# Row loads held until the MLP passes, five more x blocks by crossbar in batches 1 and 2, and a reordered front for batch 0

## The chip, the cores and the metric

The kernel runs on one NeuronCore of a Trainium2 chip. The metric is device time in microseconds (us). One NeuronCore has TensorE (PE, matrix products into PSUM), VectorE (DVE), ScalarE (ACT), GpSimd (POOL), SyncE (SP), each with its own in-order instruction queue, and 16 DMA engines that the queues share. Here GpSimd issues all loads from memory (software descriptors), and SP issues the outputs, small copies between on-chip tiles, and the transposes by the DMA crossbar.

## What is computed

Two stages, one after the other. First, chunked attention with memory: 4 batches, 8 heads, 768 positions, head size 64. Queries come in chunks of 32; each sees 8 memory keys and the keys from 16 before the chunk to 8 behind it.

```python
for c in range(nc):                                  # 24 chunks of 32
    q_c   = q[:, :, c*32 : c*32 + 32]
    k_ctx = k[:, :, max(0, c*32 - 16) : min(S, c*32 + 40)]
    scores = scale * q_c @ concat([mem_k, k_ctx]).T
    a = softmax(scores)
    out[:, :, chunk] = a @ concat([mem_v, v_ctx])
```

Second, on x, the attention's output as 3072 tokens of 512 values, an MLP with a "snake" activation:

```python
h = x @ w_in                       # 512 -> 2048
s = sin(alpha * h)
g = h + s * s / (alpha + 1e-9)
out = g @ w_out                    # 2048 -> 512
```

## The kernel before

One batch at a time goes through an attention stage and an MLP pass, and the second matmuls of a batch (by w_out) are fed, piece by piece, into the stages of the next one.

**Attention.** Keys and queries lie transposed in `kTs` and `qTs`, two buffers that alternate by batch; values lie in `vws`, alternating too. A block `j` is 96 queries (three chunks) with 128 keys: 16 before, 40 more, 8 memory keys, 64 more. For batches 1 to 3 `attention` runs the blocks 0 to 7: `scores` (TensorE, then three Exp instructions on ScalarE), two steps later `values` (TensorE, then `rinv` and `x_blk` on VectorE), and then the block's result is turned into `xT`. This is done by `turn_x`, four TensorE transposes and a VectorE copy, or, for the first `crossed` blocks, by one crossbar transpose on SP's queue (line 467). Before, `crossed` is 0 in batches 1 and 2 and 5 in batch 3. A number of second matmuls of the batch before, from the list `shares`, is put between the steps.

**Batch 0's front.** `attention_first` works by pairs of heads. Per pair: `turn_k`, `turn_q` (TensorE transposes and copies by ScalarE and VectorE), `sc` (scores of two halves and one Exp each), `pv` (values, `rinv`, `x_blk`) and `x` (transposes and a ScalarE copy). `warm(n)` issues n dummy matmuls on zeroes. All pairs' scores come first, then all values.

**The MLP pass.** `layer` goes through 16 steps `ft`: 8 first matmuls (line 483), Sin (line 503) on ScalarE, a square on VectorE, GpSimd or ScalarE by the letters V, P, A of a string, and the sum with h on VectorE (line 513). `second` holds the matmuls by w_out (line 529); its result is copied from PSUM into `o_sb` and sent out by SP. While `attention` runs, ScalarE makes this copy; otherwise VectorE and ScalarE take turns.

**Loads.** Batches 0 and 1 load k and q by `load_qk` and turn them on TensorE (`pair_up`, `turn`). Batches 2 and 3 load rows by `load_rows` (16 loads of k rows into `kst`, 6 of q rows into `qst`), and `cross_steps` turns each of the 14 tiles by a crossbar transpose on SP's queue into `kTs`, `qTs`. Before, the rows of batch 2 are loaded ahead of batch 1's attention, and its k tiles are crossed from that attention's fourth step on; the q tiles follow at the start of MLP pass 1. The rows of batch 3 are loaded after MLP pass 1, and all its 14 crossings are issued together in MLP pass 2 at step `ft` = 2. V of a batch is loaded just after the attention before it (`load_v`, four loads), and its memory rows are put in by eight small copies on SP (`send_memv`).

The order on every engine is the order in which the program calls; nothing is rescheduled. A load on GpSimd's queue waits for the landing of the eighth load before it.

Of the kernel before, what the change touches and what calls it, by code (L numbers as in the profile page):

```python
# [42 lines left out]
def kernel(  # L43
# [77 lines left out]
    memkT = consts.tile([P, HP, 32], BF, name="memkT")  # L121
    w_in_sb = consts.tile([P, KT, d_ff], BF, name="w_in_sb")
    w_out_sb = consts.tile([P, FT, d_model], BF, name="w_out_sb")
    ident_f = consts.tile([FT, FT], F32, name="ident_f")
    alpha_sb = consts.tile([P, FT], F32, name="alpha_sb")
    inv_alpha = consts.tile([P, FT], F32, name="inv_alpha")
# [3 lines left out]
    def alloc_qk():  # L130
        kb = qkst.tile([P, H, 6, D], BF, name="k_bf")
        qb = qkst.tile([P, H, 6, D], BF, name="q_bf")
        return kb, qb

    def load_rows(b):
        for j in range(NJ):
            lo = QW * j - 16
            r0 = max(0, -lo)
            nc.gpsimd.dma_start(  # L139
                kst[r0:64, j, :].rearrange("p (h d) -> p h d", d=D),  # L140
                k[b, :, lo + r0:lo + 64, :].rearrange("h p d -> p h d"),
            )
            n = min(56, S - (QW * j + 48))
            nc.gpsimd.dma_start(  # L144
                kst[72:72 + n, j, :].rearrange("p (h d) -> p h d", d=D),
                k[b, :, QW * j + 48:QW * j + 48 + n, :].rearrange("h p d -> p h d"),
            )
        nc.sync.dma_start(
            kst[64:72], memk_st[64:72, b - 2, :].unsqueeze(1).to_broadcast([NM, NJ, H * D])
        )  # L150
        for t in range(NSUB):
            nc.gpsimd.dma_start(  # L152
                qst[:, t, :].rearrange("p (h d) -> p h d", d=D),
                q[b, :, P * t:P * t + P, :].rearrange("h p d -> p h d"),
            )

    def cross_steps(b):
        for j in range(NJ):
            nc.sync.dma_start_transpose(kTs[b % 2][:, :, P * j:P * j + P], kst[:, j, :])
            yield  # L160
        for t in range(NSUB):
            nc.sync.dma_start_transpose(qTs[b % 2][:, :, P * t:P * t + P], qst[:, t, :])  # L162
            yield

    def load_qk(b, bufs, h0, h1):
        for src, dst in ((k, bufs[0]), (q, bufs[1])):
# [4 lines left out]

    def load_v(b, parts=((0, H),)):
        vw = vws[b % 2][:].rearrange("p h j c -> p (h j) c")
        vf = v[b].rearrange("h (j t) d -> t (h j) d", t=QW)
        n = H * NJ
        if len(parts) > 1:
            load_v_edges(vw, vf, n)
        for h0, h1 in parts:
            c0, c1 = h0 * NJ, h1 * NJ
            nc.gpsimd.dma_start(vw[16:64, c0:c1, 0:D], vf[0:48, c0:c1])  # L180
            nc.gpsimd.dma_start(vw[72:120, c0:c1, 0:D], vf[48:96, c0:c1])
        if len(parts) == 1:
            load_v_edges(vw, vf, n)

    def load_v_edges(vw, vf, n):
        nc.gpsimd.dma_start(vw[0:16, 1:n, 0:D], vf[80:96, 0:n - 1])
        nc.gpsimd.dma_start(vw[120:128, 0:n - 1, 0:D], vf[0:8, 1:n])

    def put_memv(b, eng, h0, h1):
        eng.tensor_copy(  # L190
# [188 lines left out]
    def attention_first(kq, alphas, ahead):  # L379
        xT = xp.tile([P, KT, S], BF, name="xT")  # L380
        pt, xb = {}, {}

        def turn_k(hp):
            t = turn(kq[0], hp, None)
            put_k(0, hp, t)
            put_k_edges(0, hp, t)

        def turn_q(hp):
            put_q(0, hp, turn(kq[1], hp, None))

        def sc(hp):
            for half in range(2):
                pt[hp, half] = unit_scores(hp, half)

        def pv(*u):
            xb[u] = unit_values(*u, pt[u])

        def x(*u):
            unit_turn(xT, *u, xb.pop(u))

        turn_k(0)
        warm(2)
        turn_q(0)
        mt = packed(single(), HP, 32)
        for g in range(HP):
            nc.tensor.transpose(mt[:, g, :], memk_bf[0:32, 2 * g:2 * g + 2, :].rearrange("p e d -> p (e d)"), ident[0:32, 0:32])
        nc.vector.tensor_copy(memkT[:], mt)
        put_memk(0)
        warm(3)
        turn_k(1)  # L410
        warm(2)
        sc(0)
        turn_q(1)
        alphas()
        put_memv(0, nc.vector, 0, H)
        warm(2)
        turn_k(2)
        warm(2)
        sc(1)
        turn_q(2)  # L420
        turn_k(3)
        warm(4)
        turn_q(3)
        sc(2)
        warm(2)
        sc(3)
        nc.scalar.preload_act_table(ACTF.Sin)
        send_memv(1)
        plan(big=(4, 0, 2), one=(6, 7))
        units = [(hp, half) for hp in range(HP - 1) for half in range(2)]  # L430
        pv(0, 0)
        for n in range(1, len(units)):
            warm(1)
            pv(*units[n])
            warm(1)
            x(*units[n - 1])
        warm(1)
        pv(3, 0)
        x(2, 1)
        pv(3, 1)  # L440
        x(3, 0)
        ahead(0, 0, xT)
        ahead(1, 0, xT)
        x(3, 1)
        ahead(2, 0, xT)
        return xT
# [73 lines left out]
    def second(i, gT, cut=0):  # L520

        def begin_o():
            bank = take_bank("one")
            kept.add(bank)
            return bank

        def part(s, bank, f0, f1):
            for ft in range(f0, f1):
                nc.tensor.matmul(  # L529
                    ps[:, bank, :], gT[:, ft, P * s:P * s + P], w_out_sb[:, ft, :],  # L530
                    start=(ft == 0), stop=(ft == FT - 1),
                )
                if ft < FT - 1:
                    yield

        def end_o(s, bank):
            kept.remove(bank)
            rings["one"].remove(bank)
            rings["one"].append(bank)
            o_sb = mlp.tile([P, d_model], F32, name="o_sb", bufs=2)  # L540
            if s % 2 == 0 and not state["attending"]:
                nc.vector.tensor_copy(o_sb[:], ps[:, bank, :])  # L542
            else:
                nc.scalar.copy(o_sb[:], ps[:, bank, :])  # L544
            nc.sync.dma_start(out[S * i + P * s:S * i + P * s + P, :], o_sb[:])

        early = []
        if cut:
            for s in range(2):
                early.append(begin_o())  # L550
                yield from part(s, early[s], 0, cut)
        for s in range(NSUB):
            bank = early[s] if s < len(early) else begin_o()
            yield from part(s, bank, cut if s < len(early) else 0, FT)
            end_o(s, bank)
            yield
# [15 lines left out]
        nc.vector.memset(vw[96:128, H - 1, NJ - 1, 0:D], 0.0)  # L572
    load_qk(0, kq, 0, 2)
    masks.make_identity(nc, ident[:])
    for hp in range(1, HP):
        load_qk(0, kq, 2 * hp, 2 * hp + 2)
    load_v(0, [(2 * hp, 2 * hp + 2) for hp in range(HP)])
    nc.gpsimd.dma_start(memv_st[64:72, 1:B].rearrange("n b h d -> n (b h) d"),
                        mem_v[1:B].rearrange("b h n d -> n (b h) d"))
    for kT in kTs:  # L580
        nc.vector.memset(kT[:, :, 0:16], 0.0)
        nc.vector.memset(kT[:, :, 848:856], 0.0)
# [37 lines left out]
    xT = attention_first(kq, alphas, ahead)  # L620
    for c in range(2):
        load_w_out(c)
    kq1 = alloc_qk()
    load_qk(1, kq1, 0, H)
    for bb in range(2):
# [29 lines left out]
    def begin_0(ft):  # L655
        if ft == 3:
            plan(h=[6] + rings["big"])
        if ft == 11:
            load_v(1)
        if ft == 15:  # L660
            prs.extend(pair_up(kq1[0], n) for n in range(3))

    layer(0, xT, "VPPAPAVPPAPAVAAA", begin_0, 0)
    last4 = rings["h"]
# [2 lines left out]
    feed.take(20)  # L667
    for pc in range(2 * HP):
        hp = pc % HP
        if pc + 3 < 2 * HP:  # L670
            prs.append(pair_up(kq1[(pc + 3) // HP], (pc + 3) % HP))
        t = turn(None, hp, prs[pc])
        if pc < HP:
            put_k(1, hp, t)
            put_k_edges(1, hp, t)
        else:
            put_q(1, hp, t, hp % 2 == 1)
        feed.take(2)
    nc.scalar.preload_act_table(ACTF.Exp)
    feed.take(4)  # L680
    load_rows(2)
    crossings = cross_steps(2)
    xT = attention(1, feed, (6, 8, 4, 4, 4, 3, 3, 3, 3, 1, 1), 2, 0, crossings, 3)
    load_v(2)
    send_memv(2)

    for i in range(1, B):
        last = i == B - 1
        if i > 1:
            crossings = cross_steps(i + 1) if not last else iter(())  # L690

        def begin(ft, i=i):
            if ft == (2 if i > 1 else 0):
                for _ in crossings:
                    pass

        if i == 1:
            assert feed.left() == 16
# [5 lines left out]
            plan(h=rings["big"])  # L704
            layer(i, xT, "AAAV", begin, feed.left() - (0 if last else 16))
        if not last:
            if i + 2 < B:
                load_rows(i + 2)
            plan(big=rings["h"])
            nc.scalar.preload_act_table(ACTF.Exp)  # L710
            feed.take(6)
            xT = attention(i + 1, feed, (4, 8, 4, 4, 3, 3, 3, 3, 4, 4, 4), 2, 5 if i == B - 2 else 0)
            if i + 2 < B:
                load_v(i + 2)
                send_memv(i + 2)
    feed.take(200)


# [28 lines left out]
```

The softmax here doesn't subtract the row's maximum and nothing guards it: scores larger than these inputs give would overflow.

## Time and profile before

| | |
|---|---|
| median of 6 runs | 226.04 us (225.82 to 226.6) |
| the profiled execution | 225.83 us, span 224.0 us |
| TensorE busy | 212.0 us (95%) |
| ScalarE busy | 152.4 us (68%) |
| VectorE busy | 132.9 us (59%) |
| GpSimd busy | 84.4 us (38%) |
| granted TensorE clock | 0.997 on average |

Times in the profile count from the span's start. The stages of batch 0's front end at about 27 us, MLP pass 0 at 49, the attention of batch 1 at 76, of batch 2 at 116, of batch 3 at 164; the last second matmuls run to 220. A line such as "L483 PE MATMUL ps<-xT,w_in_sb" names a line of the kernel, the engine, the operation, the tile written and those read. In the list of waits, "PE ps L483 <- DVE gT L513: 1.5, 5, 0.5" says that TensorE's line 483 waited for VectorE's line 513 for 1.5 us in all, 5 times, at most 0.5. Busy times of TensorE are modelled from the starts of its matmuls, and a few per cent of its records are missing, so busy is not the same as full speed.

### The profile page before, as it was taken

The numbers are of one execution on the slowest core, as the hardware profiler recorded it, in microseconds if no ns is written. First come the engines' busy times: TensorE is split into PE (matmuls) and PEld (weight loads), VectorE is DVE, ScalarE is ACT, GpSimd is POOL, SyncE is SP. The second block draws the span as 40 slices with busy tenths as digits, with TensorE's granted clock in tenths as the row PEclk, the third lists the DMA queues.
The fourth block names the chain that finished last, engine by engine and source line by source line (L and its number), as shares of the span: only waits on it lengthen the run. The fifth ranks groups of instructions, "written<-read, shape, count | busy, mean of one in ns | idle before, by whom it ended". The sixth has DMA issues, their size and how long they took to land.

```text
span 224.0 us, 4432 instructions
## 1 busy us (share of the span) xinstructions
PE 212.0 (95%) x1694; PEld 115.8 (52%) x1720; DVE 132.9 (59%) x234; ACT 152.4 (68%) x226; POOL 84.4 (38%) x106
## 2 busy tenths in 40 slices
PE   7998999999998999999999999999999999999992
PEld 2555555555545655554665555544555555544440
DVE  5684748793516869995682875756644863861110
ACT  2559478894787689999846879798929678651011
POOL 7969743796989941184980000000000000000000
PEclk9999999999999999999999999999999999999998
DMA  5999999999999999999999945542230110111211
GB/s 80 169 128 141 191 208 206 205 201 126 111 206 113 175 123 173 100 142 113 168 183 108 86 95 108 104 142 82 60 111 0 50 47 0 48 51 47 94 68 72
DMA packets 94573, 25.97 MB, mean 116 GB/s; under 512 B 82632, under 2 KB 91480, under 8 KB 94552
## 3 DMA queue, kind: packets, MB, share of 16 engines
q0 software_dynamic: 71520, 14.81, 113.6%
q1 hardware_dynamic: 23032, 10.88, 23.2%
q8 instruction: 13, 0.21, 0.5%
q14 instruction: 8, 0.07, 0.1%
HBM read 29.67 MB, written 6.29 MB: 161 GB/s over the span
## 4 chain that ended last, share of the span: by engine, by line
PE 66%; DVE 10%; ACT 7%; DMA 6%; issue 4%; SPq 3%; POOL 1%; DVEq 0%; ACTq 0%; POOLq 0%
PE ps L529 31%; PE ps L483 22%; DVE gT L513 6%; SPq L162 3%; ACT u L503 3%; DVE u L510 3%; DMA kT<-kst 3%; PE ps L296 3%; PE ps L270 2%; PE ps L323 2%; DMA q_bf<-in_q_dram 2%; PE ps L234 1%; PE ps L328 1%; PE ps L313 1%; ACT u L507 1%
## 5 line engine op out<-in xcount | busy, mean ns | idle before, releaser
L529 PE MATMUL ps<-w_out_sb,gT 128*128 128x512 bf16 x362 | 94.6, 379 | 1.5 <-ACT o_sb L544 0.4
L483 PE MATMUL ps<-xT,w_in_sb 128*128 128x384 bf16 x512 | 91.2, 326 | 1.6 <-DVE gT L513 1.5
L513 DVE SCALAR_TENSOR_TENSOR gT<-u,inv_alpha,ps 128x768 bf16<-128x768 f32 x64 | 63.3, 1012 | 24.0 <-ACT u L507 20.0
L483 PEld LDWEIGHTS <-w_in_sb 128*128 128x128 bf16 x512 | 49.6, 98 | 39.0 <-issue 3.2
L503 ACT ACTIVATE u<-ps,alpha_sb 128x768 f32<-128x768 f32 x64 | 56.6, 895 | 18.5 <-PE ps L483 17.6
L529 PEld LDWEIGHTS <-gT 128*128 128x128 bf16 x384 | 34.3, 98 | 30.9 <-issue 0.9
L507 ACT ACTIVATE u<-u 128x768 f32<-128x768 f32 x40 | 33.7, 843 | 1.2
L283 ACT ACTIVATE pt<-ps,biasm 128x256 bf16<-128x256 f32 x72 | 28.6, 480 | 5.0 <-ACT pt L283 2.6
L544 ACT COPY o_sb<-ps 128x512 f32<-128x512 f32 x16 | 9.4, 589 | 25.5 <-PE ps L529 25.5
L510 DVE TENSOR_TENSOR u<-u 128x768 f32<-128x768 f32 x18 | 17.2, 954 | 6.0 <-ACT u L503 6.0
L542 DVE COPY o_sb<-ps 128x512 f32<-128x512 f32 x8 | 5.5, 690 | 20.0 <-PE ps L529 17.2
L303 DVE TENSOR_TENSOR x_blk<-ps,rinv 96x512 bf16<-96x512 f32 x24 | 16.5, 687 | 0.8
L144 POOL DMA_DIRECT2D kst<-in_k_dram x16 | 11.7, 731 | 11.3 <-DMA vw<-in_v_dram 4.5
L302 DVE RECIPROCAL rinv<-ps 96x8 f32<-96x8 f32 x24 | 4.9, 203 | 17.0 <-ACT pt L283 10.7
L323 PE MATMUL ps<-idle 128*128 128x512 bf16 x35 | 12.0, 429 | 1.6 <-DVE vw L571 1.2
L139 POOL DMA_DIRECT2D kst<-in_k_dram x16 | 11.1, 694 | 6.2 <-DMA vw<-in_v_dram 5.2
L249 ACT COPY kT<-ps 128x672 bf16<-128x672 bf16 x8 | 5.7, 719 | 9.4 <-PE ps L234 6.6
L510 POOL TENSOR_TENSOR u<-u 128x768 f32<-128x768 f32 x6 | 8.9, 1494 | 6.9 <-ACT u L503 6.9
L296 PEld LDWEIGHTS <-pt 128*128 128x128 bf16 x192 | 9.0, 98 | 4.6 <-issue 0.7
L152 POOL DMA_DIRECT2D qst<-in_q_dram x12 | 10.5, 899 | 0.4 <-DMA kst<-in_k_dram 0.3
L296 PE MATMUL ps<-vw,pt 128*128 128x65 bf16 x192 | 9.8, 193 | 0.4 <-DMA kT<-kst 0.2
L316 DVE COPY xT<-ps 128x384 bf16<-128x384 bf16 x19 | 6.6, 348 | 4.3 <-PE ps L313 4.3
(77 smaller groups left out, 152.3 us busy)
## 6 DMA issues: line engine op xcount, KB each, us to landing
out_dram<-o_sb SPq DMA_DIRECT2D x24, 256.0 KB
vw<-in_v_dram POOLq DMA_DIRECT2D x6, 384.0 KB, 13.7
w_out_sb<-in_moe_w_out_dram POOLq DMA_DIRECT2D x2, 1024.0 KB, 18.0
w_in_sb<-in_moe_w_in_dram POOLq DMA_DIRECT2D x3, 512.0 KB, 9.7
qst<-in_q_dram POOLq DMA_DIRECT2D x12, 128.0 KB, 6.2
kst<-in_k_dram POOLq DMA_DIRECT2D x14, 64.0 KB, 5.9
kst<-in_k_dram POOLq DMA_DIRECT2D x14, 56.0 KB, 6.1
k_bf<-in_k_dram POOLq DMA_DIRECT2D x4, 192.0 KB, 5.1
```

The source lines that it names most:

```text
L139: nc.gpsimd.dma_start(kst[r0:64, j, :].rearrange("p (h d) -> p h d", d=D), k[b, :, lo + r0:lo + 64, :].rearrange("h p d -> p h d"),)
L144: nc.gpsimd.dma_start(kst[72:72 + n, j, :].rearrange("p (h d) -> p h d", d=D), k[b, :, QW * j + 48:QW * j + 48 + n, :].rearrange("h p d -> ...
L283: nc.scalar.activation(pt[:, 0:H * QW].rearrange("p (g e c) -> p g e c", g=2, e=4)[:, :, :, 32 * m:32 * m + 32], sc[:, :, 0:4 * QW].rearra ...
L296: nc.tensor.matmul(otv[:, e, hp, :], pt[:, QW * i:QW * i + P], vws[b % 2][:, 2 * hp + e, j, 0:D + 1],)
L303: nc.vector.tensor_tensor(out=x_blk[:].rearrange("p g e d -> p e g d"), in0=otv[0:QW, :, :, 0:D], in1=rinv[:].unsqueeze(3).to_broadcast([Q ...
L323: nc.tensor.matmul(z, idle[:, 0:P], idle[:])
L483: nc.tensor.matmul(hT[:, hf, 0:HALF], w_in_sb[:, kt, P * ft:P * ft + P], xT[:, kt, HALF * hf:HALF * hf + HALF], start=(kt == 0), stop=(kt ...
L503: nc.scalar.activation(u[:], hT[:, :, 0:HALF], ACTF.Sin, scale=alpha_sb[:, ft:ft + 1])
L507: nc.scalar.activation(u[:], u[:], ACTF.Square)
L510: eng.tensor_tensor(out=u[:], in0=u[:], in1=u[:], op=ALU.mult)
L513: nc.vector.scalar_tensor_tensor(out=gT[:, ft, :].rearrange("p (e c) -> p e c", e=2), in0=u[:], scalar=inv_alpha[:, ft:ft + 1], in1=hT[:, ...
L529: nc.tensor.matmul(ps[:, bank, :], gT[:, ft, P * s:P * s + P], w_out_sb[:, ft, :], start=(ft == 0), stop=(ft == FT - 1),)
```

## The change

- **Front of batch 0.** V of heads 0 and 1 is loaded before k and q of heads 4 to 7. The values of pair 0 and of the first half of pair 1 are put between the scores of pairs 1 to 3; there are 8 fewer dummy matmuls (31 for 39); the memory rows of V are copied earlier.
- **V.** A load covers the part before the memory rows and the part behind them whole, so a full V is two loads for four (three for batch 3). V of batch 2 is loaded before batch 1's attention, V of batch 3 at the start of MLP pass 1. The memory rows of batches 1 and 2 are sent from step 11 of MLP pass 0; the load of `memv_st` goes behind those of w_out.
- **Rows.** The rows of batches 2 and 3 are loaded at the start of MLP passes 1 and 2, behind a one-element copy on GpSimd (`gate`) that reads the last column of x block 5, in the order in which the blocks need them. Crossings follow the same order; in MLP pass 2 one is issued per step.
- **Crossbar.** `crossed` is 5 in batches 1, 2 and 3.
- **o_sb.** While `attention` runs, VectorE makes all these copies.
- **Pairs of batch 1.** Four `pair_up` copies are made ahead instead of three.

```diff
+    order = ((0, 0), (1, 1), (2, 2), (3,), (4, 3), (5, 4), (6, 5), (7,))
     def load_rows(b):
-        for j in range(NJ):
+        for jt in order:
+            j = jt[0]
...
+            for t in jt[1:]:
+                nc.gpsimd.dma_start(
+                    qst[:, t, :].rearrange("p (h d) -> p h d", d=D),
+                    q[b, :, P * t:P * t + P, :].rearrange("h p d -> p h d"),
+                )
...
     def cross_steps(b):
-        for j in range(NJ):
+        for jt in order:
+            j = jt[0]
             nc.sync.dma_start_transpose(kTs[b % 2][:, :, P * j:P * j + P], kst[:, j, :])
             yield
-        for t in range(NSUB):
-            nc.sync.dma_start_transpose(qTs[b % 2][:, :, P * t:P * t + P], qst[:, t, :])
-            yield
+            for t in jt[1:]:
+                nc.sync.dma_start_transpose(qTs[b % 2][:, :, P * t:P * t + P], qst[:, t, :])
+                yield
...
+            part(0, 64, -16, c0, c1)
+            c0, end = h0 * NJ, 0
+            if b == B - 1 and h1 == H:
+                c1 -= 1
+                end = 1
+            part(72, 128, 48, c0, c1)
...
+        put_memv(0, nc.vector, 0, H)
         warm(2)
         sc(0)
         turn_q(1)
         alphas()
-        put_memv(0, nc.vector, 0, H)
-        warm(2)
-        turn_k(2)
-        warm(2)
+        warm(3)
         sc(1)
+        t2 = turn(kq[0], 2, None)
+        put_k(0, 2, t2)
+        pv(0, 0)
+        put_k_edges(0, 2, t2)
         turn_q(2)
-        turn_k(3)
-        warm(4)
+        warm(1)
+        pv(0, 1)
+        t3 = turn(kq[0], 3, None)
+        put_k(0, 3, t3)
+        warm(1)
+        x(0, 0)
+        sc_half(2, 0)
+        put_k_edges(0, 3, t3)
         turn_q(3)
-        sc(2)
-        warm(2)
+        sc_half(2, 1)
+        x(0, 1)
+        warm(1)
+        plan(big=(4, 0, 2))
+        pv(1, 0)
         sc(3)
-        nc.scalar.preload_act_table(ACTF.Sin)
-        send_memv(1)
-        plan(big=(4, 0, 2), one=(6, 7))
-        units = [(hp, half) for hp in range(HP - 1) for half in range(2)]
-        pv(0, 0)
+        units = [(hp, half) for hp in range(1, HP - 1) for half in range(2)]
         for n in range(1, len(units)):
-            warm(1)
             pv(*units[n])
             warm(1)
             x(*units[n - 1])
+            if n == 1:
+                nc.scalar.preload_act_table(ACTF.Sin)
+            warm(1)
...
-            if s % 2 == 0 and not state["attending"]:
+            if s % 2 == 0 or state["attending"]:
                 nc.vector.tensor_copy(o_sb[:], ps[:, bank, :])
...
-    for hp in range(1, HP):
-        load_qk(0, kq, 2 * hp, 2 * hp + 2)
-    load_v(0, [(2 * hp, 2 * hp + 2) for hp in range(HP)])
+    load_qk(0, kq, 2, 4)
+    load_v(0, ((0, 2),))
+    load_qk(0, kq, 4, 6)
+    load_qk(0, kq, 6, 8)
+    load_v(0, ((2, 4), (4, 6), (6, 8)))
...
         if ft == 11:
             load_v(1)
+            send_memv(1)
+            send_memv(2)
...
+    load_v(2)
     feed.take(4)
-    load_rows(2)
-    crossings = cross_steps(2)
-    xT = attention(1, feed, (6, 8, 4, 4, 4, 3, 3, 3, 3, 1, 1), 2, 0, crossings, 3)
-    load_v(2)
-    send_memv(2)
+    xT = attention(1, feed, (6, 8, 4, 4, 4, 3, 3, 3, 3, 1, 1), 2, 5)
...
         def begin(ft, i=i):
-            if ft == (2 if i > 1 else 0):
+            if i == 1 and ft == 0:
+                nc.gpsimd.tensor_copy(gate[:], xT[0:1, 0, QW * 6 - 1:QW * 6])
+                load_rows(2)
+                load_v(3)
                 for _ in crossings:
                     pass
+            if i == 2:
+                if ft == 0:
+                    nc.gpsimd.tensor_copy(gate[:], xT[0:1, 0, QW * 6 - 1:QW * 6])
+                    load_rows(3)
+                if ft >= 1:
+                    next(crossings, None)
...
-            xT = attention(i + 1, feed, (4, 8, 4, 4, 3, 3, 3, 3, 4, 4, 4), 2, 5 if i == B - 2 else 0)
-            if i + 2 < B:
-                load_v(i + 2)
-                send_memv(i + 2)
+            xT = attention(i + 1, feed, (4, 8, 4, 4, 3, 3, 3, 3, 4, 4, 4), 2, 5)
+            if i == 1:
+                send_memv(3)
```

## The prediction

> **What bounds the kernel now.** I read the page's busy table and slices first, then TensorE's list of waits, then the engines' busy time by stage, then the timeline of the stages that the change touches.
>
> ```profile
> PE 212.0 (95%) x1694; PEld 115.8 (52%) x1720; DVE 132.9 (59%) x234; ACT 152.4 (68%) x226; POOL 84.4 (38%) x106
> PE   7998999999998999999999999999999999999992
> ```
> TensorE is busy for 212.0 of 224.0 us, with only the first and last slices thin. A change pays here if it takes work off TensorE, or shortens a stretch where TensorE is filled with dummy matmuls.
>
> ```profile
> PE ps L483 <- DVE gT L513: 1.5, 5, 0.5
> PE ps L313 <- ACT o_sb L544: 0.6, 1, 0.6
> PE ps L529 <- ACT o_sb L544: 0.4, 1, 0.4
> ```
> These waits of TensorE, with a few of 0.5 us and less, are all there is after 27 us: no wait for a load is on the path, so moving loads gains almost nothing by itself.
>
> ```profile
> 19.00:27.00 8.00, 7.03 (x113) 4.78 (x112) 6.78 (x16) 5.57 (x10) 7.76 (x10) 1.00 1.85 168
> 76.00:102.00 26.00, 24.87 (x159) 13.99 (x158) 22.56 (x28) 22.28 (x28) 11.88 (x16) 1.00 2.54 135
> ```
> (Stage, length, busy PE, PEld, DVE, ACT, POOL, granted clock, DMA share, GB/s.) In the end of batch 0's front VectorE carries 6.78 of 8.00 us and TensorE's business is partly dummies. In batch 1's MLP VectorE is close to the bound (22.56 of 26), so that pass can only start earlier, not run faster.
>
> **The change, part by part.**
>
> *Five x blocks of batches 1 and 2 by crossbar.* Each block loses 4 TensorE transposes and one VectorE copy of 0.34 us. Batch 3 already does this and has the same feed counts as batch 2, so the trace holds the comparison:
>
> ```profile
> 104.39 0.34 PE L270 MATMUL ps<-qT,kT 64*128 64x96 bf16 x8
> 120.08 0.90 ACT L503 ACTIVATE u<-ps,alpha_sb 128x768 f32<-128x768 f32 x1 [2.00 <-PE ps L483]
> 153.10 0.34 PE L270 MATMUL ps<-qT,kT 64*128 64x96 bf16 x8
> 167.72 0.90 ACT L503 ACTIVATE u<-ps,alpha_sb 128x768 f32<-128x768 f32 x1 [2.00 <-PE ps L483]
> ```
> From the third block's scores to the first Sin: 15.69 us in batch 2, 14.62 in batch 3. The difference, 1.07 us, is my price for five blocks; twice gives **-2.14**. By issue gaps alone 4 transposes take 0.17 us, so 10 blocks would give -1.7; with every block at its full 0.34 it is -3.4. I keep both as ends.
>
> The new wait is the crossbar's landing. Block 3's crossing is issued when its x_blk is ready: 72.3 before, less some 2.1, is 70.2. Its reader, the layer's first matmuls, came at 76.18 and comes at about 74.0: 3.8 us of slack. Two rows give the landing:
>
> ```profile
> 155.32 6.51 SPq L467 DMA_TRANSPOSE xT<-x_blk  x4
> 66.02 6.30 DMA kT<-kst
> ```
> In batch 3, with a quiet queue, four crossings take 6.5 us of the queue with their waits, and no matmul waits for one. At 66.02, amid row loads, one crossing took 6.30 us. In the changed kernel the row loads are held until block 5 is turned, so only V(2) is in flight in batch 1's attention (V(1) landed by 62, V(2) behind it by about 70: 7,600 rows at the rate above take 7 to 8 us) and V(3) in batch 2's. I take 0, and 2.5 us per batch for the rival.
>
> *o_sb copies in attention move from ScalarE (0.59) to VectorE (0.69).* Nine move. VectorE has 9.0 of 14 us busy in batch 2's attention and loses five 0.34 copies, so it has room. One place is on the path: in batch 1 the last fed matmul ended at 78.07 and block 7's xT copy ran on VectorE at 78.25; the o_sb copy now sits ahead, 78.07 + 0.69 = 78.76: **+0.5**. In batches 2 and 3 the same copy fits before block 7 (117.50 + 0.69 against 118.83).
>
> *Batch 0's front.* Four fewer dummy matmuls before the scores and four in the unit loop are no gain by themselves; VectorE's chain sets the end:
>
> ```profile
> 19.62 0.20 DVE L361 RECIPROCAL rinv<-ps 96x8 f32<-96x8 f32 x1 [2.65 <-PE ps L355]
> 26.11 0.19 DVE L361 RECIPROCAL rinv<-ps 96x8 f32<-96x8 f32 x1
> 29.64 3.50 ACT L503 ACTIVATE u<-ps,alpha_sb 128x768 f32<-128x768 f32 x4 [0.82 <-PE ps L483]
> ```
> All eight units' normalisations run behind the last scores: 7 steps in 6.49 us, 0.93 each, then 3.53 us to the first Sin. After the change three units run between the scores. Against that, V of heads 0 and 1 (about 1,900 rows of 256 B; by the landing events the later V parts took 0.7 us for 768 such rows) goes ahead of k and q of heads 4 to 7: +2.0 us. k of heads 4, 5 landed at 11.0 by the landing events, now 13.0; q 14.1; the next k 15.0, q 16.5. Then: k turned 13.1, its ScalarE copy to 14.5, edges behind the first x_blk to 15.25, q copy (0.95) to 16.2, scores of pair 2 and Exp to 17.9, pair 3's q copied by 18.5, second half's scores to 18.4, unit (1,0) at 18.6, pair 3's scores 18.9 to 20.4, unit (1,1) at 20.4 and its reciprocal at 20.8. Four more steps of 0.93 to 1.06 (the widest before, x_blk starts at 20.70 and 21.76): 24.5 to 25.0, against 26.11: **-1.3**. If the early V part lands as slowly as the first V loads did (3,048 rows from 14.5 to 18.4, so 2.4 us) and starts 1 us late, it is -0.4; at best -1.9. The granted clock is 1.00 in these stages; TensorE's gaps grow from 0.34 to some 0.7 us.
>
> *MLP 0.* The loads in front of GpSimd's first square now wait for w_in's fourth part: up to +0.5, I take **+0.2**. w_in and w_out land up to 0.9 us earlier (memv_st goes behind them); no matmul waited for them.
>
> *memv sends for batches 1 and 2* move to MLP 0's tail: 16 at 0.75 on SP, about 44 to 56, ahead of the first output at 58.86: nothing. *V loads* shrink from four DMAs to two or three; GpSimd's 4.3 us of issue (44.9 to 49.15) shortens, hidden behind 4.4 us of second matmuls.
>
> *Row loads and crossings.* The gate is one element copied on GpSimd (under the 0.83 us that a whole pair copy takes there); behind it queue only loads (MLP 1 to 3 have no GpSimd squares). Batch 2's 22 loads took 17 us to issue (57.5 to 74.5) and some 6 to land; from 74.3 they are in by 97 to 100. SP's 14 crossings at 1.3 (18.2 us) end at 99 to 102. Block 0 is needed at about 98, block 7 at 108: hidden; without that cover each late microsecond counts whole. In MLP 2 one crossing per step replaces 14 in a row, which held an output and so VectorE (2.78 us before the o_sb copy at 149.32); TensorE lost only 0.23 us by it: **-0.25**.
>
> Sum: -2.14 + 0.5 - 1.3 + 0.2 - 0.25 = **-3.0**. The profiled execution took 225.83 (span 224.0 and 1.8 around it), so 222.8; the median of the runs is 0.2 above it: **223.0**.
>
> **A rule against it.** The Trainium skill, "VectorE: DVE Perf Modes", section "The three transpose paths", gives a 128x128 transpose 390 ns on TensorE and 1309 ns on the crossbar. By that, as an estimate, a block of four costs 5.2 us and five in series 26 us, longer than the attention; the reader would wait some 12 us in each of two batches and the time would be near 247. The rows here price a whole block at 1.2 us of issue, and I go by them.
>
> **Rivals.**
> 1. *Crossings land late (slower).* V(2) and V(3) in flight slow each crossing as the loads did at 66.02: 6.3 us against 3.8 of slack is 2.5 us in each batch, +5.0: 223.0 + 5.0 = 228.0. It decides once the landing passes 3.8 + 1.5 = 5.3 us. For it: V(2) and the crossings overlap. Against: V(2) ends about when block 3 is issued. 0.14.
> 2. *The front gains nothing:* the late k and q eat the overlap, so 223.0 + 1.3 = 224.3; with part of the attention gain lost too, up to 225.5. 0.20.
> 3. *No net change:* ScalarE's Exp (1.2 us a block, pitch 1.25 to 1.5) paces attention, the turns were hidden, and the front is even: about 225.8. The batch 2 and 3 comparison speaks against it. 0.07.
> 4. The forecast: 221.2 to 224.0. 0.59.
>
> **How the numbers follow.** 0.2% (0.45 us) is about what can be told here from no change: below 225.6 is faster. Forecast and rival 2: 0.79 faster; rival 3: 0.06 same; slower 0.15. The low end is 226.0 less 3.4, 1.9 and 0.25, plus 0.5: 221.0. The high end takes in rivals 2 and 3: 225.9.
>
> **What would show it.** Right: 9 xT copies by VectorE where there were 19, third scores to Sin about 14.6 us in batches 1 and 2, first Sin near 28.3, no TensorE wait on xT, kT or qT. Wrong: TensorE's waits name DMA xT<-x_blk (rival 1); first Sin at 29.6 or later (rival 2); attention stages as long as before (rival 3).

## The result, and the profile after

| | median | ratio to before, 95% interval |
|---|---|---|
| before | 226.33 us (79 runs) | 1 |
| after | 225.35 us (37 runs) | 0.994 [0.9928, 0.9952] |
| predicted | 223.0 us | 0.987 |

The change makes the kernel faster by 0.6%, 1.1 to 1.6 us. The prediction had the sign, and its range holds the time, but less than half of the 3.0 us came. Ratios compare only the executions at the common speed, so they differ a little from the quotients of the medians, and the one trace of an execution outside it (v3_late, 309 us at a granted clock of 0.657) is not read. The profiled execution of after took 226.07 us (span 224.3), 0.7 above the median of its runs, while that of before (225.83) lay 0.5 below its own. So the trace shows where the time goes, and the ratios say how much.

The page's busy row and TensorE's slices, and then TensorE's list of waits (total, times, longest):

```profile
PE 209.3 (93%) x1647; PEld 112.6 (50%) x1672; DVE 136.6 (61%) x233; ACT 147.9 (66%) x217; POOL 82.6 (37%) x102
...
PE   7989799989999899999799999999999999999991
```
```profile
PE ps L508 <- DVE gT L538: 1.5, 5, 0.5
...
PE ps L508 <- DMA xT<-x_blk: 1.0, 2, 0.6
PE ps L283 <- DMA qT<-qst: 1.0, 1, 1.0
PE ps L554 <- DVE gT L538: 0.8, 1, 0.8
```
Forty transposes and eight dummy matmuls are gone (part of the lower PE figure is missing records: act_pad below, the same on TensorE, shows 211.7), but the span is no shorter. The two waits for a DMA (L508 is the first matmul, L283 the scores) are new: before, the longest wait for one was 0.2 us. The 0.8 us at L554, the second matmul, behind VectorE's gT was not in the list.

The engines by stage (length, PE, PEld, DVE, ACT, POOL, clock, DMA share, GB/s), for the same two stretches:

```profile
19.00:27.00 8.00, 6.80 (x101) 4.20 (x101) 5.26 (x12) 5.67 (x10) 5.67 (x7) 1.00 1.45 196
76.00:102.00 26.00, 24.44 (x159) 13.71 (x158) 22.40 (x26) 22.01 (x27) 19.36 (x24) 1.00 1.92 146
```
The front's end is lighter on VectorE (5.26 us for 6.78), and batch 1's MLP is as VectorE-bound as it was (22.40 for 22.56). The timeline, third scores and first Sin of batches 2 and 3:

```profile
103.83 0.34 PE L283 MATMUL ps<-qT,kT 64*128 64x96 bf16 x8
...
120.06 0.90 ACT L528 ACTIVATE u<-ps,alpha_sb 128x768 f32<-128x768 f32 x1 [5.19 <-PE ps L508]
...
152.77 0.34 PE L283 MATMUL ps<-qT,kT 64*128 64x96 bf16 x8
...
167.16 0.90 ACT L528 ACTIVATE u<-ps,alpha_sb 128x768 f32<-128x768 f32 x1 [4.64 <-PE ps L508]
```
Batch 2 was to fall from 15.69 us to 14.62. It rose to 16.23. The chain of waits says why, in the same stretch:

```profile
100.70 9.58 DMA qT<-qst
110.44 5.47 DMA xT<-x_blk
```
A q crossing was issued at 100.70 and landed 9.58 us later, the crossing of x block 3 5.47 us after its issue. The prediction's row for a crossing amid loads was 6.30 us. A crossing tells of its landing by sixteen updates of its semaphore, and these are in the trace for every crossing; counted to the last update, the five x blocks of batch 2 landed 8.43, 7.14, 6.57, 5.47 and 5.71 us after their issue, those of batch 1 4.54, 3.53, 2.36, 2.33 and 2.37.

The stages of each kernel, as differences of starts in its trace (us): first scores to first Sin of batch 0; that Sin to the first second matmul; first scores to first Sin in batches 1, 2 and 3; last o_sb copy's end to the span's end. Only the stages that moved are listed; the MLP passes 1 and 2 and the last stretch keep their lengths within 0.02 us between before and after. The span is printed to 0.1 us, so the tails hold within 0.05. Each row is one execution; that of memk_early took 226.98 us, 1.7 above its median.

| | front | MLP 0 | att. 1 | att. 2 | att. 3 | tail |
|---|---|---|---|---|---|---|
| before | 20.39 | 19.28 | 18.51 | 19.32 | 18.27 | 3.36 |
| after | 19.78 | 19.89 | 18.03 | 19.87 | 17.74 | 4.21 |
| old_front | 20.40 | 19.46 | 17.89 | 19.91 | 17.76 | 3.41 |
| no_crossbar | 19.34 | 19.80 | 18.38 | 19.73 | 17.73 | 4.10 |
| memk_early | 19.13 | 19.54 | 17.37 | 21.86 | 17.74 | 4.17 |
| v3_memk | 19.14 | 19.42 | 17.64 | 18.07 | 17.73 | 4.35 |
| v3_memk_osb | 19.13 | 19.81 | 17.03 | 18.26 | 18.96 | 3.26 |
| v3_memk_turn | 19.75 | 19.85 | 18.39 | 19.73 | 17.73 | 3.98 |
| v3_memk_pad | 19.13 | 19.55 | 17.24 | 18.41 | 17.73 | 3.23 |
| quiet_square | 19.31 | 19.28 | 20.59 | 18.38 | 17.74 | 3.31 |
| before_osb | 20.39 | 19.28 | 18.39 | 19.73 | 18.05 | 3.47 |

### The profile page after: what moved, and what is told of

Read it like the earlier page. It is cut to its first block, busy times and chain, and to the rows that moved or that the text cites. A ratio compares the mean times of both kernels' runs of the same rounds, so it can differ in the third digit from the quotient of the medians.

```text
span 224.3 us, 4352 instructions
## 1 busy us (share of the span) xinstructions
PE 209.3 (93%) x1647; PEld 112.6 (50%) x1672; DVE 136.6 (61%) x233; ACT 147.9 (66%) x217; POOL 82.6 (37%) x102
## 4 chain that ended last, share of the span: by engine, by line
PE 60%; DMA 12%; POOL 7%; DVE 6%; SPq 5%; ACT 4%; issue 3%; DVEq 0%; ACTq 0%; POOLq 0%
PE ps L554 31%; PE ps L508 23%; DMA qT<-qst 4%; DMA q_bf<-in_q_dram 4%; SPq L164 3%; DMA xT<-x_blk 2%; SPq L167 2%; PE ps L283 2%; DVE gT L538 2%; DMA kst<-in_k_dram 2%; ACT u L528 2%; PE ps L309 2%; POOL kst L148 1%; POOL qst L153 1%; POOL kst L143 1%
## 5 line engine op out<-in xcount | busy, mean ns | idle before, releaser
L554 PE MATMUL ps<-w_out_sb,gT 128*128 128x512 bf16 x362 | 94.7, 380 | 1.8 <-DVE gT L538 0.8
L508 PE MATMUL ps<-xT,w_in_sb 128*128 128x384 bf16 x512 | 91.3, 326 | 2.8 <-DVE gT L538 1.5
L508 PEld LDWEIGHTS <-w_in_sb 128*128 128x128 bf16 x512 | 49.5, 98 | 40.7 <-issue 5.4
L554 PEld LDWEIGHTS <-gT 128*128 128x128 bf16 x384 | 34.3, 97 | 31.9 <-issue 1.5
L567 DVE COPY o_sb<-ps 128x512 f32<-128x512 f32 x17 | 11.7, 689 | 25.3 <-PE ps L554 24.7
L535 DVE TENSOR_TENSOR u<-u 128x768 f32<-128x768 f32 x18 | 17.8, 987 | 6.0 <-ACT u L528 5.9
L183 POOL DMA_DIRECT2D vw<-in_v_dram x15 | 18.1, 1213 | 0.3 <-issue 0.3
L316 DVE TENSOR_TENSOR x_blk<-ps,rinv 96x512 bf16<-96x512 f32 x24 | 16.5, 687 | 1.7 <-DMA xT<-x_blk 0.7
L569 ACT COPY o_sb<-ps 128x512 f32<-128x512 f32 x7 | 4.1, 584 | 19.0 <-PE ps L554 19.0
L336 PE MATMUL ps<-idle 128*128 128x512 bf16 x28 | 9.7, 451 | 1.8 <-DVE vw L596 1.2
L535 POOL TENSOR_TENSOR u<-u 128x768 f32<-128x768 f32 x6 | 8.9, 1493 | 5.2 <-ACT u L528 5.2
L283 PEld LDWEIGHTS <-kT 64*128 64x128 bf16 x192 | 4.9, 94 | 11.6 <-issue 11.0
```

What stands on the lines that cost most here:

```text
L183: nc.gpsimd.dma_start(vw[p0:p1, c0:c1, 0:D], flat[r0:r0 + QW * (c1 - c0)].rearrange("(n t) d -> t n d", t=QW)[0:p1 - p0],)
L316: nc.vector.tensor_tensor(out=x_blk[:].rearrange("p g e d -> p e g d"), in0=otv[0:QW, :, :, 0:D], in1=rinv[:].unsqueeze(3).to_broadcast([Q ...
L508: nc.tensor.matmul(hT[:, hf, 0:HALF], w_in_sb[:, kt, P * ft:P * ft + P], xT[:, kt, HALF * hf:HALF * hf + HALF], start=(kt == 0), stop=(kt ...
L535: eng.tensor_tensor(out=u[:], in0=u[:], in1=u[:], op=ALU.mult)
L554: nc.tensor.matmul(ps[:, bank, :], gT[:, ft, P * s:P * s + P], w_out_sb[:, ft, :], start=(ft == 0), stop=(ft == FT - 1),)
```

## The experiments

The theory after the result: V of batch 3, loaded during batch 1's MLP, is still in flight in batch 2's attention and slows the crossings there; the front's gain is real. The rival: the attention is paced by ScalarE and VectorE, and the crossings are worth nothing wherever V(3) is. Ratios are to the kernel before, whose runs shared the chip.

**v3_late**: V(3) moves one MLP pass later.

```diff
                 load_rows(2)
-                load_v(3)
...
                     load_rows(3)
+                    load_v(3)
```


> The changed kernel with V of batch 3 loaded behind the rows of batch 3 in MLP pass 2 instead of behind the rows of batch 2 in pass 1. Theory (V(3) in flight makes the crossings of batch 2's rows and x blocks land late): TensorE's waits for qT, kT and xT in batch 2's attention (1.0, 0.2 and 0.4 us in the profile of the changed kernel) go, crossings land within 3 us of their issue, and the time falls by 1.2 to 2 us, to about 223.7. Rival (the crossings are late because they start late, behind the copy of the memory keys): they still start at about 83 and the wait for qT stays near 1 us; the time falls by 0.4 at most.

Measured 224.25 us, ratio 0.9883 [0.9851, 0.9914], 0.57% better than after: V(3) takes 1.3 us. v3_memk below gives a trace with V(3) moved.

**memk_early**: the small copy of batch 2's memory keys into `kst`, which goes ahead of the crossings on SP's queue, is issued in MLP 0 (a new function `load_memk`, called behind `send_memv(2)`). In after, the first crossing waited 4.2 us for that copy and left at 83.4, not at 80.

> The changed kernel with the memory keys of batch 2 copied into the row tile at step 11 of MLP pass 0 instead of just ahead of the crossings. Theory of the late start: the first crossing goes out at about 79 to 80 instead of 83.4, the last at about 99, the wait for qT in batch 2's attention goes, and the time falls by about 1.1 us. Theory of V(3) in flight: the last crossings still land late (they meet V(3) from 97 on), the wait for qT shrinks but the one for xT (0.4) stays; the time falls by 0.5 to 1.

Measured 225.24 us, 0.9969 [0.9943, 0.9996]: no gain over after. In the trace the wait on qT is gone, and another has taken its place (waits, chain):

```profile
PE ps L512 <- DMA xT<-x_blk: 2.0, 1, 2.0
```
```profile
109.22 5.97 DMA xT<-x_blk
```
So the late start of the crossings was not the cause by itself: with V(3) in flight, the next crossing is late. The forecast of 0.5 to 1.1 us was missed.

**no_crossbar**: `crossed` is 0 in batches 1 and 2, all else as after.

> The changed kernel with the five x blocks of batches 1 and 2 turned on TensorE again; everything else is kept. By the prediction's term the crossbar is worth 2.1 us less 0.5, so this is 1.6 us slower than the changed kernel. By the theory that late landings took most of it back, it is 0.3 to 1.0 us slower. By the rival that it is worth nothing here, equal.

Measured 226.06 us, 0.998 [0.9955, 1.0004]. With V(3) in flight the crossings of batches 1 and 2 together are worth 0.4%, 0.9 us, of the 2.14 in the sum. (The expectation takes off 0.5 for the o_sb copies, but these are on VectorE in both kernels.)

**old_front**: the front and the load order of before (its `turn_k`, `sc`, `pv` order and its `load_qk`, `load_v` lines), all else as after.

> The changed kernel with batch 0's loads and instruction order as before (V after all k and q, all scores before all values), the rest as changed. By the prediction's term 1.3 us slower than the changed kernel; by the first Sin of the profiled execution (28.95 against 29.64) 0.7 slower; by the theory that MLP pass 0 gives it back (its second matmuls started at 48.84 against 48.92) equal.

Measured 226.03 us, 0.9997 [0.9968, 1.0026]. The difference is 0.57%, 1.3 us, the term of the sum, but it is not the front's alone: in old_front's trace the tail is 0.8 us shorter than in after (3.41 for 4.21), for a reason found below. Without that the front would be worth some 2 us by the ratios, while front and MLP 0 together are as long in the trace of after as in that of before, and 1.1 us shorter in that of v3_memk. No run isolates the front.

**v3_memk, v3_memk_turn, v3_memk_osb, v2_early.** v3_memk has V(3) late and memory keys early. Each of the others adds one edit to it: `crossed` 0 in batches 1 and 2 (v3_memk_turn), the o_sb copies of the attention on ScalarE (v3_memk_osb), V(2) issued earlier (v2_early).

```diff
# v3_memk_osb
-            if s % 2 == 0 or state["attending"]:
+            if s % 2 == 0 and not state["attending"]:
# v2_early
             prs.extend(pair_up(kq1[n // HP], n % HP) for n in range(4))
+            load_v(2)
...
-    load_v(2)
     feed.take(4)
```


> The changed kernel with V of batch 3 loaded in MLP 2 behind the row loads, and the memory keys' rows of batch 2 copied in MLP 0. Theory 1 (loads in flight on the shared DMA engines make the crossbar transposes land late, V(3) above all): ratio to before 0.985 to 0.989, some 223 us; with V(3) out of the way, TensorE's waits on qT and xT in batch 2's attention (1.00 and 0.39 us in the changed kernel) are gone, layer 2's first matmul starts at 114.2 to 115.1 where it started at 116.05, and the xT crossings land in 2 to 3 us. Theory 2 (batch 2's attention is paced by ScalarE's Exp and VectorE, and the late landings are beside it): first matmul at 115.8 to 116.2 and a ratio of 0.992 to 0.995 as in the changed kernel.

Measured 223.67 us, 0.9906 [0.9869, 0.9943], between the ranges of the two theories; the trace decides for the first. Third scores and first Sin of batch 2 (timeline):

```profile
102.88 0.34 PE L287 MATMUL ps<-qT,kT 64*128 64x96 bf16 x8
...
117.32 0.90 ACT L532 ACTIVATE u<-ps,alpha_sb 128x768 f32<-128x768 f32 x1 [4.69 <-PE ps L512]
```
That is 14.44 us, against 16.23 in after; the prediction had 14.6. The same stretch of batch 2 in windows, after first and then v3_memk (columns as above):

```profile
104.00:110.00 6.00, 5.32 (x76) 2.64 (x72) 3.73 (x10) 5.02 (x13) 0.00 (x0) 1.00 1.96 104
```
```profile
104.00:110.00 6.00, 5.89 (x87) 2.96 (x87) 4.45 (x11) 5.24 (x14) 0.00 (x0) 1.00 0.37 94
```
The DMA share (the time of all packets over that of 16 engines, above 1 where packets overlap) falls from 1.96 to 0.37, and TensorE is busy for 5.89 of 6 us instead of 5.32. No wait on qT or kT is left; that on xT is 0.2 us in all. The five x blocks of batch 2 land 2.29, 2.30, 2.40, 3.88 and 2.96 us after their issue. The Trainium skill, "DMA: Bandwidth & Descriptors", section "Queues, rings and completion order", says that each DMA engine takes turns between the queues that have work for it, packet by packet; these rows agree in that crossings on SP's queue land late beside a load on GpSimd's. They do not isolate it, since a crossing also has earlier crossings ahead of it: in after the last k crossing, issued at 102.09, landed at 111.88, behind the issue of four x crossings (106.36 to 110.44); in v3_memk it was issued at 98.60 and landed at 102.68, before the first.

> As the run before (V(3) late, memory keys early), but the five blocks of batches 1 and 2 turned by TensorE again. With V(3) in flight this cost 0.4% (ratio 0.998 against 0.994). Theory 1: the crossbar's price of -2.14, less 0.5 for the o_sb copy that stays, is there once V(3) is out of the way, so this kernel is 1.0 to 1.6 us slower than the run before, ratio 0.992 to 0.996. Theory 2 (the turns were hidden): within 0.4 us of the run before.

Measured 226.42 us, 1.0007 [0.9982, 1.0032], so the crossings are worth 1.0%, 2.3 us, when V(3) is away, against 0.9 us with V(3) there. The rival falls. And without crossings of x blocks, moving V(3) and the memory keys gains nothing (0.998 in no_crossbar, 1.0007 here; attention 2 takes 19.73 us in both), so V(3) costs time through these crossings.

> V(3) late, memory keys early, and the o_sb copies of the attention stages on ScalarE as before the change. The prediction priced VectorE's copies at +0.5 in batch 1. If that price is right, this is 0.2 to 0.5 us faster than the run with the copies on VectorE. If ScalarE's Exp paces the attention (theory 2), nine copies of 0.59 on ScalarE cost up to 1 us instead, and TensorE waits on ACT o_sb again as it did before the change (0.6 and 0.4 us).

Measured 222.72 us, 0.9837 [0.981, 0.9864], 0.7% better than v3_memk, more than expected. Its trace puts the gain in an odd place: the last o_sb copy ends later than in v3_memk (217.94 against 217.35), the span earlier (221.2 against 221.7). What is shorter is the tail, 3.26 us against 4.35.

> V(3) late, memory keys early, and V(2) issued behind the first four pair copies on GpSimd (at about 50.7 where it was 57.1). Theory 1: V(2) is in by about 67, before the first x block's crossing, so the crossings of batch 1 land in 2 to 3 us, TensorE's wait of 0.62 us on xT at 75.24 goes, layer 1's first matmul starts at 74.2 to 74.7, and the ratio is 0.981 to 0.987. Rival: the wait at 75.24 is the crossings' own issue on SP (1.2 to 1.3 us each, in line behind each other), and stays at 0.4 to 0.7; the ratio is that of the run without this edit.

Measured 225.70 us, 0.9987 [0.9959, 1.0015]: worse than v3_memk by 0.8%. The wait at layer 1 stayed, at 0.35 us, as the rival here said: SP was behind already. The rival's equal time did not come: nothing was won, and the later pair copies wait behind V(2)'s issue on GpSimd: a wait of 0.6 us on batch 1's kT is new. The rest of the 0.8% I can't place.

**The tail.** A DMA view of the last 4.3 us, in 40 slices: GB/s, then queues with packets, MB and share of time; after, then act_pad:

```profile
GB/s 0 0 0 0 0 0 0 0 95 286 438 362 400 324 362 96 0 19 38 0 38 19 19 19 0 0 0 0 0 0 0 0 0 0 0 0 0 0 0 0
...
q1 hardware_dynamic: 144, 0.26, 16.3%
q14 instruction: 1, 0.01, 1.1%
```
```profile
GB/s 0 0 0 0 0 0 0 0 0 0 0 0 0 0 0 0 0 133 362 457 362 362 362 343 57 0 0 0 0 0 0 0 0 0 0 0 0 0 0 0
...
q1 hardware_dynamic: 144, 0.26, 16.3%
```
q1 holds the last output's packets, q14 is a fetch of 8 KB of instructions. In after it falls 0.2 us behind the start of that output, and a thin trail of packets, one behind the other, follows the block by 0.8 us: 1.65 us from first to last, 0.83 before. The fetch is one packet of 0.75 us (221.13 to 221.88), and the trail, eight packets of 2 KB, starts when it ends. In act_pad no fetch is there and no trail. By the traces ScalarE is the engine: with 217 operations on its row of the page the last fetch falls 0.2 to 2.9 us behind the last output's start (after, v3_memk, v3_memk_turn, old_front, before_osb), with 226 it falls 20 to 23 us ahead of it (before, v3_memk_osb, act_pad). In the fifteen traces read here the last output takes 1.41 to 1.96 us in the six where a fetch falls 0.2 us behind its start, and 0.82 or 0.83 in the other nine. The change took nine copies from ScalarE. To test it, nine copies of 16x8 were added while ScalarE idles at the start.

```diff
+    for _ in range(9):
+        nc.scalar.copy(pad[:], idle[0:16, 0:8])
     xT = attention_first(kq, alphas, ahead)
```
**act_pad** (on after):

> The changed kernel with nine tiny copies (16x8) added on ScalarE at the start, where it idles. Seen so far: in the profiles of the changed kernel an 8 KB instruction fetch falls at 220.7 us, beside the last output's packets, which then take 1.65 us instead of 0.82, and the span ends 4.2 us after the last o_sb copy instead of 3.4; where ScalarE has its nine o_sb copies back, the fetch falls at 198.5. Theory A: the nine copies that ScalarE lost put its last fetch there. Then the fetch falls at 195 to 205 here, the tail after the last o_sb copy is 3.3 to 3.5 us, and the ratio is 0.989 to 0.992. Theory B (the fetch does no harm or belongs to another engine): tail 4.0 to 4.4, ratio 0.993 to 0.996.

Measured 224.49 us, 0.9912 [0.9884, 0.9941], tail 3.28 us. The last fetch falls at 198.1.

**v3_memk_pad** (on v3_memk):

> V(3) late, memory keys early, o_sb on VectorE, and the nine tiny copies on ScalarE. With o_sb on ScalarE this version had 0.9837, without it 0.9906. Theory A: the pad alone brings 0.985 to 0.988, since most of that difference was the tail (4.35 us after the last o_sb copy against 3.26). Theory B: 0.990 to 0.992, since the difference was VectorE's copies.

Measured 222.71 us, 0.9834 [0.9794, 0.9874], tail 3.23. It equals v3_memk_osb, so the o_sb copies on VectorE cost nothing in the end, and the tail was the difference. The fetch is worth 0.9 to 1.1 us in the traces; the ratios give 0.6 us on after, 1.6 on v3_memk, with wide intervals.

**osb_act** (after, with o_sb on ScalarE, which also moves the fetch):

> The changed kernel with the o_sb copies of the attention stages on ScalarE as before the change; V(3) still loaded in batch 1's MLP. Theory A (tail): ratio 0.988 to 0.991, of which 0.003 to 0.004 is the tail and the rest the prediction's +0.5 for VectorE's copy in batch 1. Theory B: only the +0.5, 0.991 to 0.994. If ScalarE's Exp paces the attention: 0.994 or more.

Measured 225.11 us, 0.9947 [0.9915, 0.998], inconclusive: the tail is 3.36 us, but attention 2 with V(3) in flight took 20.26 us in this trace. By the number alone this is the case in which Exp paces the attention; v3_memk_osb, with V(3) away, speaks against it.

**before_osb** (the kernel before, with o_sb on VectorE in the attention):

> The kernel before the change with one line of it: the o_sb copies of the attention stages on VectorE. Theory A (tail): ScalarE's program is nine copies shorter, so its last instruction fetch falls beside or behind the last output; if beside, the last output takes 1.4 to 2.0 us and the span ends 4.0 to 4.4 us after the last o_sb copy (3.36 in the kernel before); if behind it, 3.4. From the second score of batch 3 on, the attention is 0.5 us shorter (17.74 from first score to first Sin against 18.27), batches 1 and 2 are 0 to 0.5 longer. Sum: ratio 0.999 to 1.006. Rival: the copy on VectorE is a gain by itself in all three batches, tail or not: ratio under 0.998.

Measured 226.01 us, 0.9986 [0.9966, 1.0006]. Here the fetch fell 2.9 us behind the start of the last output, and the tail is 3.47: nothing lost. Attention 3 is 18.05 us, 0.2 shorter and not 0.5. So nine copies fewer do not by themselves put the fetch on the output: with the same 217 operations it falls at 221.1 in after and at 224.4 here.

**MLP 0.** TensorE's 0.75 us ahead of the second matmuls waits for VectorE's gT, which is late because a square (L535, the product of u with itself) took 1.55 us beside GpSimd's issue of V(1); before, it took 0.95. Two versions moved that issue: **v1_behind** (on v3_memk_osb) behind the first pair copies, and **quiet_square** (on v3_memk_pad) with the pair copies also held until gT of step 12 is written (the `gate` line is its alone).

```diff
-            load_v(1)
             send_memv(1)
...
+            nc.gpsimd.tensor_copy(gate[:], gTs[0][0:1, 12, 0:1])
             prs.extend(pair_up(kq1[n // HP], n % HP) for n in range(4))
+            load_v(1)
```


> V(3) late, memory keys early, o_sb on ScalarE, and V(1) issued on GpSimd behind the first four pair copies (at about 50.7 where it was 44.2). Theory: VectorE's last square of MLP 0 (0.95 us before the change, 1.2 to 1.55 beside the V load's issue) is back at 0.95, TensorE's gap ahead of the second matmuls (0.7 us in that version) is 0.2 or less, and the ratio is 0.980 to 0.983. Rival: the gap is set by ScalarE's own last squares and stays, or V(1) lands behind 65 us and batch 1's first values wait; ratio 0.983 to 0.988.

Measured 224.68 us, 0.9918 [0.9887, 0.9948]. The square still took 1.33 us, now beside the pair copies, and batch 1 paid for the later V(1) with a wait of 1.32 us on xT. The forecast (a square of 0.95 us, 0.980 to 0.983) failed.

> The version with V(3) late, memory keys early and the pad, with GpSimd kept idle beside VectorE's last square of MLP 0: the pair copies wait for the finished step 12 and V(1) is issued behind them. Theory: the square takes 0.95 us as in the kernel before (1.2 to 1.55 in the others) and TensorE's gap ahead of the second matmuls of batch 0 is 0.2 us or less (0.4 to 0.75 in the others). Rival: square and gap stay. The time itself should be worse than 0.9834, 0.988 to 0.994, since V(1) and V(2) then load beside the crossings of batch 1: a wait of 1 to 2 us on xT at layer 1's first matmul.

Measured 225.87 us, 0.9969 [0.9937, 1.0001], worse than the 0.988 to 0.994 expected. The timeline around the square, after and then quiet_square:

```profile
44.17 3.35 POOL L183 DMA_DIRECT2D vw<-in_v_dram  x2
...
46.12 1.55 DVE L535 TENSOR_TENSOR u<-u 128x768 f32<-128x768 f32 x1
...
48.84 1.46 PE L554 MATMUL ps<-w_out_sb,gT 128*128 128x512 bf16 x5 [0.75 <-DVE gT L538]
```
```profile
45.72 0.95 DVE L540 TENSOR_TENSOR u<-u 128x768 f32<-128x768 f32 x1
...
47.84 2.32 PE L559 MATMUL ps<-w_out_sb,gT 128*128 128x512 bf16 x9
...
75.53 0.81 PE L513 MATMUL ps<-xT,w_in_sb 128*128 128x384 bf16 x4 [1.90 <-DMA xT<-x_blk]
```
With GpSimd idle the square takes 0.95 us, the gap is gone, and MLP 0 is 19.28 us long, as before. The last row is the price: V(1) and V(2) now load beside batch 1's crossings, and TensorE waits 1.90 us for one. This is V(3)'s effect made on purpose in the other batch. The Trainium skill, "SBUF — State Buffer", section "SBUF: two separate sides", says that a VectorE operation with two inputs in SBUF and a GpSimd operation that reads SBUF shut each other out of a shared pair of ports; the square reads two such inputs, and 1.33 us beside pair copies against 0.95 beside nothing agrees. Beside the issue of loads the traces differ (0.95 in before, 1.08 to 1.55 in the versions of after), and why stays open.

**The best version** of those run is v3_memk_pad: 222.71 us, 0.9834 of before and 1.1% below after.

## Why the prediction was right or wrong

- *x blocks by crossbar, -2.14, and o_sb, +0.5.* The price was right and the cover was not. With V(3) away (v3_memk against before) attention 1 and 2 fall by 0.87 and 1.25, together 2.12, with o_sb on VectorE included; by the ratios the crossings are worth 2.3. In after, attention 1 falls by 0.48 and attention 2 rises by 0.55. The +0.5 for o_sb in batch 1 did not come: with that edit alone (before_osb) attention 1 changes by -0.1, attention 2 by +0.4 and attention 3 by -0.2, and the time is that of before (0.9986).
- *The step that failed: "I take 0" for late landings.* For batch 2 the prediction named V(3) as in flight and still took the quiet rows (6.5 us for four, which is their issue; no quiet landing was read). Its row amid loads, 6.30 us, was the low end: in the same trace the eight k crossings of batch 2 landed 6.4 to 9.3 us after their issue. Rival 1's condition, a landing of more than 5.3 us, was met by all five x blocks of batch 2 (5.47 to 8.43) and not by block 3 of batch 1 (2.33), so the rival's mechanism is what happened, in one batch of the two. Its size was 2.5 us a batch; moving V(3) away gained 1.3 (0.994 to 0.9883) and 1.4 (0.9969 to 0.9906). The loads themselves were "hidden" by their landing times alone: V(3) landed at 104 to 115 and is read after 150, so nothing in the sum priced it. The crossings of batch 2's rows were counted on SP's queue (14 at 1.3 us, out by 99 to 102; the last left at 102.09), and their landing, 9.8 us for the last, was left out.
- *The slack of 3.8 us in batch 1* was taken from when x_blk would be ready. The rows of after:

```profile
66.96 3.78 SPq L492 DMA_TRANSPOSE xT<-x_blk  x2
...
70.47 0.69 DVE L316 TENSOR_TENSOR x_blk<-ps,rinv 96x512 bf16<-96x512 f32 x1
70.84 0.54 SPq L570 DMA_DIRECT2D out_dram<-o_sb  x1
71.47 3.81 SPq L492 DMA_TRANSPOSE xT<-x_blk  x3
...
75.24 0.81 PE L508 MATMUL ps<-xT,w_in_sb 128*128 128x384 bf16 x4 [0.62 <-DMA xT<-x_blk]
```
Block 3's x_blk is ready at 71.16, not 70.2. Its crossing is the second of the three from 71.47, each some 1.3 us, so it leaves at 72.77: SP was held by the second crossing, issued with V(2) in flight (2.33 us), and by an output. TensorE was ready at 74.62. The slack was 1.85 us, and a landing with no load in flight is 2.31 (the same crossing in v3_memk), so some wait was certain:

```profile
71.85 2.31 DMA xT<-x_blk
```
- *Front, -1.3:* right in sign, and by the ratios in size (old_front, 0.57%), but the tail has a part in that ratio, so the agreement may be luck. The first Sin of after came at 28.95, between the 28.3 forecast and the 29.6 of rival 2. In the traces with the new front the first Sin is 0.6 to 1.26 us nearer to the first scores; q3 landed at 17.2 for the 16.5 assumed.
- *MLP 0, +0.2:* mis-sized, +0.1 to +0.6, and by another mechanism: the cost is not at GpSimd's first square but at VectorE's last, beside GpSimd's work. V's load was said to be hidden behind second matmuls, and its effect on VectorE was not asked for.
- *MLP 2, -0.25:* nothing came; the pass took 29.37 us before and 29.36 after.
- *Attention 3*, held even, fell by 0.53; with o_sb on ScalarE it is longer (18.96 in v3_memk_osb against 17.73 in v3_memk), so by these two traces the move that was priced as a cost gained there. *The tail*, not in the sum, cost some 0.8 in the profile.
- *The 1309 ns a transpose of the Trainium skill* ("VectorE: DVE Perf Modes", section "The three transpose paths"), by which the time would be near 247: the whole block's crossing, 2.31 us from issue to landing, is less than half of the 5.2 us estimated for four transposes; the rows were the better guide.
- *The chances* of the closing lines, 0.06 for same and 0.15 for slower, are 0.07 and 0.14 in the list of rivals; nothing else rests on the difference.

Without V(3) beside the crossings and with the fetch out of the tail the change gives 222.7 us (0.9834, 3.7 us less than before), where the sum had 3.0 less. V(3) takes about 1.3 us and the fetch 0.6 to 1.1 us, more than the miss of 1.4 to 1.9; attention 3's 0.5 and the o_sb cost that did not come lie against them, MLP 0 and MLP 2 beside them. The split is not exact, as most executions of after scatter from 223.2 to 226.3 us, and the profiled one, with 226.07, lies near the upper end.

## What to carry to other kernels

A transfer is not hidden because its own reader is far away: ask which short transfers with near readers run beside it. Time the reader's slack from when the queue lets the transfer go, not from when its data is ready, and add a landing measured in the traffic it will meet. When a change trims an engine's program and the trace's tail grows, look at the last output's packets and what shares them.

## What was not expected of the hardware

- An instruction fetch of 8 KB beside the last output's packets makes that output 1.4 to 2.0 us long instead of 0.82, and its place moves with the number of ScalarE's operations; nine copies of 16x8 at an idle moment took 0.9 to 1.1 us off the tail.
- A crossing of a 96x512 block with no load in flight mostly landed 2.3 to 2.4 us after its issue (up to 4.2 us in the traces of before and v3_memk_pad), and in batch 2 of after, with V(3) in flight and earlier crossings not yet landed, after 5.5 to 8.4 us; there a crossing of k rows took up to 10.06.
- An instruction fetch may delay a crossing too: in v3_memk_pad fifteen of the sixteen updates of block 3 of batch 2 had come 3.0 us after its issue and the last at 4.20, with two fetches (16 KB and 8 KB, at 110.8 and 110.9) beside its packets. No run isolates this.
- An elementwise product of two SBUF operands on VectorE took 0.95 us with GpSimd idle and up to 1.55 with GpSimd at work.
